# Full attention: the second of two passes over each group of exp pieces moves from VectorE to GpSimd

## The chip, the cores and the metric

The kernel runs on one core of one Trainium2 chip. The metric is the device time of one execution in microseconds (us), as a median over runs. Before the change it is 1766.3 us (3 runs, 1759.68 to 1770.49).

Engine names in the profile: PE is TensorE (PEld its weight loads), DVE is VectorE, ACT is ScalarE, POOL is GpSimd, SP is SyncE.

## The reference

Four layers alternate, each with a layer norm in front and a residual: a sliding local attention (A) and a full attention with one shared key/value head (B). The change touches only B:

```python
def _B_ref(x, wq, wk, wv, wo):          # S = 2048, D = 512, H = 32, Dh = 16
    q = (x @ wq).reshape(B, S, H, Dh)   # ... transposed to heads first
    k = x @ wk                          # one head for all
    v = x @ wv
    scores = einsum("bhqd,bkd->bhqk", q, k) * (Dh ** -0.5)
    p = softmax(scores, axis=-1)
    o = einsum("bhqk,bkd->bhqd", p, v)
    return (...) @ wo
# x = x + A(norm(x)); x = x + B(norm(x)); and both once more
```

Each B layer needs 32 x 2048 x 2048 exponentials. On 128 partitions that is 2048 pieces of 512 columns a layer, 4096 in all.

## The kernel before

TensorE writes scores to PSUM, the memory in which this kernel's matmuls leave their results. Two engines share the exponentials:

- ScalarE takes two pieces in one exp instruction (1024 columns), and TensorE multiplies each by the values: two matmuls a piece (score, value).
- VectorE makes a cheap exponential from bit patterns. A *copy* clamps the score, adds a bias and stores it as int16, and these bits, read as fp16, are roughly 2^x. For four pieces together (a *group*, 2048 columns) two *passes* add a constant to those int16 numbers. TensorE then multiplies the copy and both pass results by values with three different weights, and the sum is a good exponential. A VectorE piece costs four matmuls (a score, three values).

```python
NJ = 3
J_OFF = (0.0, OCT / 3, 2 * OCT / 3)          # OCT = 1024
...
class AttnB:
    def exp(self, key, slot, pt, n):
        self.chain("act", self.nc.scalar.activation(out=self.pt[pt][:, 0:n, :], in_=self.st.pop(key)[:, 0:n, :],
                                                    func=AF.Exp, scale=E_SCALE))
    def copy(self, bank, buf, r):
        self.chain("dve", self.nc.vector.tensor_scalar(out=self.t[buf][:, r, :].bitcast(I16), in0=self.dv[bank][:],
                                                       scalar1=-U_BIAS, scalar2=U_BIAS, op0=ALU.max, op1=ALU.add))
    def do_pass(self, buf, out, j, n):
        self.chain("dve", self.nc.vector.tensor_scalar(out=self.i[out][:, 0:n, :].bitcast(I16),
                                                       in0=self.t[buf][:, 0:n, :].bitcast(I16), scalar1=J_OFF[j],
                                                       scalar2=None, op0=ALU.add))
```

Who takes which piece, and the order on every engine, is fixed when the kernel is built. A planner walks through the stage with a table of durations, always issues what can start first, and `chain` pins the planned order. The durations are constants in the source:

```python
class Stream:
    def copy(self, s, _):
        ...
        S.run("dve", s, 600.0)
        ...
        if len(self.filling) == self.GROUP or ...:
            for j in range(1, NJ):
                self.passes.append((s + 600, buf, j, tiles))
    def do_pass(self, s, _):
        _, buf, j, tiles = self.passes.pop(0)
        t = 133.5 * n + 66
        S.run("dve", s, t)
        ...
```

So the planner decides how many pieces go to ScalarE and how many to VectorE. If a duration in the table is wrong, the kernel stays correct, but the division and the order are wrong.

## Time and profile before

| | before |
|---|---|
| median time | 1766.3 us |
| two full-attention stages (first to last pass) | 670 + 663 us |
| VectorE / ScalarE busy, of 550 us inside the first stage | 536.7 / 531.5 us |
| exp instructions; copies; passes (VectorE / GpSimd) | 1382; 1332; 668 / 0 |

The head of the page (busy time, share of the span, instructions) and its part 4, the chain that ended last:

```profile
span 1772.6 us, 39835 instructions
PE 1569.5 (89%) x16214; PEld 539.7 (30%) x16281; DVE 1535.8 (87%) x2565; ACT 1507.3 (85%) x1721; POOL 206.2 (12%) x257
...
DVE 59%; PE 26%; ACT 9%; issue 3%; POOL 1%; DMA 0%; DVEq 0%; SPq 0%; ACTq 0%; POOLq 0%
DVE t L1103 32%; DVE i L1107 17%; PE o L1118 9%; PE ps L882 5%; PE st L1084 4%; ACT pt L1099 4%; PE dv L1084 3%; DVE P L951 2%; DVE X L1135 2%; DVE stats L857 2%; ACT P L950 1%; PE pv L910 1%; DVE x_sb L1001 1%; PE dn L980 1%; PE o L961 1%
...
L1099 ACT ACTIVATE pt<-st 128x1024 bf16<-128x1024 f32 x1382 | 1290.7, 1094 | 48.2 <-PE dv L1084 20.4
L1103 DVE TENSOR_SCALAR t<-dv 128x512 int16<-128x512 f32 x1332 | 856.9, 680 | 11.3 <-PE dv L1084 6.2
L1107 DVE TENSOR_SCALAR i<-t 128x2048 int16<-128x2048 int16 x668 | 466.0, 698 | 11.2 <-PE o L1118 0.5
```

L1103 is the copy and L1107 the pass; together they are half of the chain, so VectorE sets the pace. The three group lines give, left of the second bar, busy time in us and the mean duration of one in ns; right of it stands the idle time before them. VectorE idles 11 us before copies and 11 us before passes. ScalarE idles 48 us before its exps, so it is close behind. Busy time is less than count times mean (for the exps 1290.7 against 1382 x 1.094 = 1512 us), because the records of consecutive instructions overlap.

The table of windows, from 250 to 800 us, inside the first full-attention stage (columns: us, then busy time and count of each engine, granted TensorE clock as a share of full speed, DMA share, GB/s):

```profile
core 0: us, PE busy (x) PEld busy (x) DVE busy (x) ACT busy (x) POOL busy (x), PEclk, DMA share, GB/s
250.00:800.00 550.00, 519.34 (x4452) 144.80 (x4458) 536.71 (x891) 531.46 (x568) 27.96 (x41) 0.94 0.06 11
```

VectorE is busy 98% of this window, ScalarE 97%. GpSimd is nearly free.

The timelines of GpSimd and VectorE near the end (start us, duration us, engine, line) show that the two engines can get in each other's way already here:

```profile
1730.74 1.27 POOL L1188 TENSOR_TENSOR onc<-X,lb 128x512 bf16<-128x512 f32 x1 [6.37 <-DMA lb<-rd]
...
1729.10 0.68 DVE L1107 TENSOR_SCALAR i<-t 128x2048 int16<-128x2048 int16 x1
1729.70 1.28 DVE L1103 TENSOR_SCALAR t<-dv 128x512 int16<-128x512 f32 x2
1731.01 1.55 DVE L1107 TENSOR_SCALAR i<-t 128x2048 int16<-128x2048 int16 x1
```

The pass at 1731.01 us lasts 1.55 us in place of 0.68. GpSimd's product had begun just before and ended at 1732.01 us; the pass ends 0.55 us after that. The trace books the wait as part of the instruction. What VectorE waits for is called the port from here on; the prediction below says what it is.

The line that I used to cost the new GpSimd work is this one, from the groups of GpSimd by shape. It is the layer norm's normalisation, `x * rstd + nmr`, two operations:

```profile
L871 POOL TENSOR_SCALAR xn<-x_bf,rstd,nmr 128x512 bf16<-128x512 bf16 x9 | 6.8, 768 | 21.8 <-issue 12.5 <-PE pT L875 8.9 <-ACT xnT L845 0.5
```

### The profile page before, as it was taken

Reading aid. Unit: us, or ns where it says so; the run is one execution under the profiler, and the core shown is the slowest. Engines: PE = TensorE matmul, PEld = TensorE weight load, DVE = VectorE, ACT = ScalarE, POOL = GpSimd, SP = SyncE. Lnnn points to the kernel's source line nnn. Section 1 sums busy time; section 2 is a strip of 40 time slices with the busy share of each in tenths; the row PEclk is TensorE's granted clock in tenths of the full one; section 3 lists DMA queues with packets and bytes.
Section 4 is the critical chain, followed back from the end, with each engine's and each line's share of the span. In section 5 each row is a group of like instructions: output and inputs, shape, how many; then the busy total and the mean of one; then the engine's idle time right before and its main releaser. Section 6 shows DMA issues by size and latency. Waiting matters only on the chain.

```text
span 1772.6 us, 39835 instructions
## 1 busy us (share of the span) xinstructions
PE 1569.5 (89%) x16214; PEld 539.7 (30%) x16281; DVE 1535.8 (87%) x2565; ACT 1507.3 (85%) x1721; POOL 206.2 (12%) x257
## 2 busy tenths in 40 slices
PE   5776799899999999999977777998999999999996
PEld 3544222222222223222345442222222222222222
DVE  6565499999999999998955646999999999999997
ACT  4654599999999989999856546999999999999994
POOL 4343000000000000000123420000000000000001
PEclk9988799999988999978998878999999899998998
DMA  4000000000000000000000000000000000000000
GB/s 123 3 2 3 0 5 12 17 11 10 12 11 11 11 11 11 11 11 11 11 2 3 2 2 1 11 11 11 11 11 23 11 11 11 23 14 11 11 15 30
DMA packets 40736, 22.96 MB, mean 13 GB/s; under 512 B 28512, under 2 KB 34272, under 8 KB 40544
## 3 DMA queue, kind: packets, MB, share of 16 engines
q1 hardware_dynamic: 39680, 18.50, 4.8%
q8 instruction: 129, 2.11, 0.5%
q10 hardware_dynamic: 864, 1.84, 0.3%
q14 instruction: 63, 0.52, 0.1%
HBM read 13.27 MB, written 2.59 MB: 9 GB/s over the span
## 4 chain that ended last, share of the span: by engine, by line
DVE 59%; PE 26%; ACT 9%; issue 3%; POOL 1%; DMA 0%; DVEq 0%; SPq 0%; ACTq 0%; POOLq 0%
DVE t L1103 32%; DVE i L1107 17%; PE o L1118 9%; PE ps L882 5%; PE st L1084 4%; ACT pt L1099 4%; PE dv L1084 3%; DVE P L951 2%; DVE X L1135 2%; DVE stats L857 2%; ACT P L950 1%; PE pv L910 1%; DVE x_sb L1001 1%; PE dn L980 1%; PE o L961 1%
## 5 line engine op out<-in xcount | busy, mean ns | idle before, releaser
L1099 ACT ACTIVATE pt<-st 128x1024 bf16<-128x1024 f32 x1382 | 1290.7, 1094 | 48.2 <-PE dv L1084 20.4
L1103 DVE TENSOR_SCALAR t<-dv 128x512 int16<-128x512 f32 x1332 | 856.9, 680 | 11.3 <-PE dv L1084 6.2
L1084 PE MATMUL st<-QT,KAB 32*128 32x512 bf16 x2764 | 560.3, 400 | 14.8 <-ACT pt L1099 13.2
L1084 PE MATMUL dv<-QT,KAB 32*128 32x512 bf16 x1332 | 512.9, 397 | 52.2 <-DVE t L1103 38.4
L1118 PE MATMUL o<-pt,VEa 128*32 128x512 bf16 x2764 | 546.3, 412 | 2.7 <-DVE t L1103 1.8
L1118 PE MATMUL o<-i,VEd 128*32 128x512 f16 x2664 | 535.7, 403 | 10.5 <-DVE i L1107 10.1
L1107 DVE TENSOR_SCALAR i<-t 128x2048 int16<-128x2048 int16 x668 | 466.0, 698 | 11.2 <-PE o L1118 0.5
L1084 PEld LDWEIGHTS <-KAB 32*128 32x128 bf16 x4096 | 188.1, 91 | 556.4 <-issue 541.5
L1118 PE MATMUL o<-t,VEd 128*32 128x512 f16 x1332 | 344.7, 407 | 0.2
L1118 PEld LDWEIGHTS <-VEd 128*32 128x32 f16 x3996 | 145.4, 94 | 225.0 <-issue 221.7
L1118 PEld LDWEIGHTS <-VEa 128*32 128x32 bf16 x2764 | 120.2, 94 | 191.9 <-issue 188.9
L753 POOL TENSOR_TENSOR chk_b<-chk_b,S 128x32 f32<-128x32 f32 x30 | 11.0, 367 | 813.6 <-DMA S<-X 684.3
L951 DVE TENSOR_TENSOR P<-P,bandmask 128x1152 bf16<-128x1152 bf16 (+1 forms) x64 | 60.9, 951 | 38.4 <-ACT P L950 37.8
L950 ACT ACTIVATE P<-s 128x1152 bf16<-128x1152 f32 (+1 forms) x64 | 71.8, 1121 | 16.7 <-PE s L945 16.6
L882 PE MATMUL ps<-xnT,w_sb 128*128 128x512 bf16 x233 | 69.2, 427 | 16.8 <-DVE k L898 8.8
L875 PE MATMUL pT<-ident,xn 128*128 128x128 bf16 x256 | 30.6, 263 | 40.4 <-ACT xn L867 23.2
L1188 POOL TENSOR_TENSOR onc<-X,lb 128x512 bf16<-128x512 f32 x30 | 39.8, 1327 | 228.2 <-DMA lb<-rd 214.5
L984 ACT ACTIVATE logs<-dn 128x512 f32<-128x512 f32 x32 | 19.1, 598 | 45.4 <-PE dn L980 45.2
L961 PE MATMUL o<-P,V 64*32 64x72 bf16 (+2 forms) x2176 | 34.9, 209 | 18.9 <-DVE P L951 15.3
L1135 DVE COPY X<-o 128x512 f32<-128x512 f32 x64 | 43.7, 683 | 8.7 <-PE o L1118 8.6
L986 DVE TENSOR_TENSOR onc<-o,rec 128x512 bf16<-128x512 f32 x32 | 22.0, 687 | 33.0 <-ACT rec L985 24.9
L747 POOL TENSOR_TENSOR logs<-logs 128x512 f32<-128x512 f32 x32 | 34.3, 1071 | 130.1 <-ACT rec L985 130.1
(108 smaller groups left out, 871.1 us busy)
## 6 DMA issues: line engine op xcount, KB each, us to landing
lb<-rd SPq DMA_DIRECT2D x240, 32.0 KB, 1.8
S<-X SPq DMA_DIRECT2D x240, 2.0 KB, 1.7
X<-X SPq DMA_DIRECT2D x120, 32.0 KB, 2.0
rd<-R SPq DMA_DIRECT2D x120, 4.0 KB, 1.5
w_sb<-in_A_wqkv_dram ACTq DMA_DIRECT2D x4, 384.0 KB, 5.6
x_bf<-in_A_x_dram SPq DMA_DIRECT2D x3, 512.0 KB, 9.3
out_dram<-xo SPq DMA_DIRECT2D x3, 512.0 KB, 3.0
x_bf<-in_A_x_dram SPq DMA_DIRECT2D x2, 256.0 KB, 5.0
```

The costliest lines, as they stand in the source:

```text
L857: nc.vector.bn_stats(out=stats[:, i, :], in_=src(i))
L882: self.nc.tensor.matmul(ps[:], lhsT=wcols(kt), rhs=xnT[:, kt, :], start=(kt == 0), stop=(kt == 3))
L950: nc.scalar.activation(out=P[:, :, 0:ncol], in_=st[:, :, 0:ncol], func=AF.Exp, scale=DH ** -0.5)
L951: nc.vector.tensor_tensor(out=P[:, :, 0:ncol], in0=P[:, :, 0:ncol], in1=self.w.band[:, 0:ncol].unsqueeze(1).to_broadcast([128, 4, ncol]), ...
L961: nc.tensor.matmul(o[32 * r:32 * r + 32, q0:q0 + w], lhsT=vv[64 * a:64 * a + 64, kb, t, gh, j, :], rhs=P[64 * a:64 * a + 64, g, col:col + ...
L1084: self.chain("pe", self.nc.tensor.matmul(out, lhsT=self.KAB[32 * g:32 * g + 32, a, kt * 128:(kt + 1) * 128], rhs=self.QT[32 * g:32 * g + 3 ...
L1099: self.chain("act", self.nc.scalar.activation(out=self.pt[pt][:, 0:n, :], in_=self.st.pop(key)[:, 0:n, :], func=AF.Exp, scale=E_SCALE))
L1103: self.chain("dve", self.nc.vector.tensor_scalar(out=self.t[buf][:, r, :].bitcast(I16), in0=self.dv[bank][:], scalar1=-U_BIAS, scalar2=U_B ...
L1107: self.chain("dve", self.nc.vector.tensor_scalar(out=self.i[out][:, 0:n, :].bitcast(I16), in0=self.t[buf][:, 0:n, :].bitcast(I16), scalar1 ...
L1118: self.chain("pe", self.nc.tensor.matmul(self.o[bank][32 * g:32 * g + 32, :], lhsT=lhsT, rhs=rhs, start=first, stop=last, tile_position=(0 ...
L1135: self.chain("dve", nc.vector.tensor_copy(out=self.X[qc, t, a][:], in_=self.o.pop(bank)[:]))
L1188: self.chain("pool", nc.gpsimd.tensor_tensor(out=self.onc[qc][:, t, :], in0=self.X[qc, t, 0][:], in1=bufs["lb"][:], op=ALU.mult))
```

## The change

The intent: VectorE bounds the stage, so take one of its two passes away. Pass 1 stays on VectorE, pass 2 runs on the idle GpSimd, ordered behind pass 1 of the same group. The planner learns a cost for GpSimd's pass (0.86 ns a column plus 250 ns: 2.01 us for a group), keeps the two kinds of pass from overlapping (`port`), gets an ageing term in its priority, and there are seven buffers for pass results in place of five. Cut to its core:

```diff
+POOL_COL = 0.86
...
-                yield (s + op.prio, s, op.ready, self.issue, (e, op))
+                yield (s + op.prio - 0.1 * (s - op.ready), s, op.ready, self.issue, (e, op))
...
-            for j in range(1, NJ):
-                self.passes.append((s + 600, buf, j, tiles))
+            self.passes.append((s + 600, buf, 1, tiles))
...
-        t = 133.5 * n + 66
-        S.run("dve", s, t)
+        t = 133.5 * n + 66 if e == "dve" else POOL_COL * 512 * n + 250
+        S.run(e, s, t)
+        self.port = s + t
+        if j < NJ - 1:
+            self.pool_passes.append((s + t + LAT["dve"], buf, j + 1, tiles))
...
-        self.i = [... for n in range(5)]
+        self.i = [... for n in range(7)]
...
+        eng = self.nc.vector if e == "dve" else self.nc.gpsimd
+        i = eng.tensor_scalar(out=self.i[out][:, 0:n, :].bitcast(I16), in0=self.t[buf][:, 0:n, :].bitcast(I16),
+                              scalar1=J_OFF[j], scalar2=None, op0=ALU.add)
+        if e == "pool":
+            order_after(self.tc, i, self.first_pass.pop(buf))
```

More of the change, by code (lines that the diff above doesn't have):

```diff
@@ L572, in __init__ @@
         self.pos = 0
-        self.exps, self.copies, self.passes = [], [], []
+        self.exps, self.copies, self.passes, self.pool_passes = [], [], [], []
+        self.port = 0.0
         self.res = res
@@ L622, in cands @@
             if self.passes:
-                s = max(S.now["dve"], self.passes[0][0], S.free_at(("i", "vec")))
+                s = max(S.now["dve"], self.passes[0][0], S.free_at(("i", "vec")), self.port)
                 if s < FAR:
-                    yield (s + (0.0 if self.run_of_copies >= 2 else B["pass"]), s, 0.0, self.do_pass, None)
+                    yield (s + (0.0 if self.run_of_copies >= 2 else B["pass"]), s, 0.0, self.do_pass, "dve")
+        elif e == "pool" and self.pool_passes:
+            s = max(S.now["pool"], self.pool_passes[0][0], S.free_at(("i", "vec")), self.port)
+            if s < FAR:
+                yield (s, s, self.pool_passes[0][0], self.do_pass, "pool")
     def fill_slot(self, s, _):
@@ L689, in copy, with do_pass @@
             self.uses[("t", buf)] = [len(tiles) + NJ - 1, 0.0, ("t", "vec")]
-            for j in range(1, NJ):
-                self.passes.append((s + 600, buf, j, tiles))
+            self.passes.append((s + 600, buf, 1, tiles))
             for r, tl in enumerate(tiles):
                 self.queue(tl, done, ("t", buf, r, 0), 1)
-    def do_pass(self, s, _):
+    def do_pass(self, s, e):
         S, io = self.s, self.io
-        _, buf, j, tiles = self.passes.pop(0)
+        _, buf, j, tiles = (self.passes if e == "dve" else self.pool_passes).pop(0)
         n = len(tiles)
-        t = 133.5 * n + 66
-        S.run("dve", s, t)
+        t = 133.5 * n + 66 if e == "dve" else POOL_COL * 512 * n + 250
[3 more added lines that the diff above has]
+            self.pool_passes.append((s + t + LAT["dve"], buf, j + 1, tiles))
         out = S.take(("i", "vec"))
         self.uses[("i", out)] = [n, 0.0, ("i", "vec")]
-        S.note(s, lambda: io.do_pass(buf, out, j, n))
-        self.run_of_copies = 0
+        S.note(s, lambda: io.do_pass(e, buf, out, j, n))
+        if e == "dve":
+            self.run_of_copies = 0
         for r, tl in enumerate(tiles):
-            self.queue(tl, s + t + LAT["dve"], ("i", out, r, j), j < NJ - 1)
+            self.queue(tl, s + t + LAT[e], ("i", out, r, j), j < NJ - 1)
         self.use(("t", buf), s + t)
@@ L1063, in __init__ @@
         self.t = [fixed.tile([128, Stream.GROUP, 512], F16, name=f"t{n}") for n in range(3)]
-        self.i = [fixed.tile([128, Stream.GROUP, 512], F16, name=f"i{n}") for n in range(5)]
+        self.i = [fixed.tile([128, Stream.GROUP, 512], F16, name=f"i{n}") for n in range(7)]
         self.NQC = S // 512
@@ L1074, in __init__ @@
         self.X, self.onc, self.onb, self.xo = {}, {}, {}, {}
-        self.sums, self.ready = {}, {}
+        self.sums, self.ready, self.first_pass = {}, {}, {}
     def chain(self, key, inst):
@@ L1104, in copy, with do_pass @@
                                                        scalar1=-U_BIAS, scalar2=U_BIAS, op0=ALU.max, op1=ALU.add))
-    def do_pass(self, buf, out, j, n):
-        self.chain("dve", self.nc.vector.tensor_scalar(out=self.i[out][:, 0:n, :].bitcast(I16),
-                                                       in0=self.t[buf][:, 0:n, :].bitcast(I16), scalar1=J_OFF[j],
-                                                       scalar2=None, op0=ALU.add))
+    def do_pass(self, e, buf, out, j, n):
+        eng = self.nc.vector if e == "dve" else self.nc.gpsimd
[3 more added lines that the diff above has]
+            order_after(self.tc, i, self.first_pass.pop(buf))
+        else:
+            self.first_pass[buf] = i
+        self.chain(e, i)
     def pv(self, bank, at, src, first, last):
```

## The prediction

> **What bounds the kernel now.** The two attention stages run (source views) from about 209 to 882 us and 1087 to 1752 us, some 1340 of 1773 us. In 250 to 800 us the table of windows shows VectorE busy 536.7 of 550 us, ScalarE 531.5, TensorE 519.3 (overlapping matmuls), GpSimd 28. The chain of waits in the second stage is nearly all VectorE: copies (L1103) 32%, passes (L1107) 17% of the span. So VectorE is first, ScalarE about 1% behind. Costs from the groups: a two-piece exp (L1099) 1290.7/1382 = 0.934 us of ScalarE; a copy 856.9/1332 = 0.643 us; a pass 466.0/668 = 0.698 us.
>
> **What changes.** From the compiled order: exps 1382 to 1340; VectorE pieces 1332 to 1416; 354 passes stay on VectorE, 354 go to GpSimd (668 on VectorE before). 84 pieces take four matmuls in place of two: +168 of 10856, 1.5%.
> - VectorE: +84 x 0.643 = +54 us, -314 x 0.698 = -219 us: -165 us. It stops being the limit.
> - ScalarE: -42 x 0.934 = -39 us (1291 to 1252). It becomes the limit. That, not the 165 us, can be gained: at the present 96 to 97% occupancy the stages take about 1300 us.
> - GpSimd: no such pass in this trace. Its 512-column tensor_scalar (L871) takes 0.768 us. The Trainium skill, "GPSIMD Engine Reference", 3.1, states 1.03 cycles per element for a body of at most two operations: 1.76 us for 2048 columns. With a fixed part fitted to L871 (0.33 us) I estimate 2.1 us, up to 2.5 us if L871's growth is steeper: about 740 of 1300 us.
>
> **The shared port.** The Trainium skill, "SBUF — State Buffer", "SBUF: two separate sides", says GpSimd and a two-port VectorE instruction lock each other out entirely. This trace agrees: the pass at 1731.01 us took 1.55 us because a GpSimd product (1.27 us) had begun at 1730.7; the median is 0.683. Copies out of PSUM never lengthened (623 to 693 ns), so they run beside GpSimd. The ordering makes VectorE's pass and GpSimd's alternate: a group has about 1300/354 = 3.67 us, the passes need 0.7 + 2.1 + hand-over, about 3.1 us.. The reciprocals (L1169), SBUF to SBUF, may now wait for GpSimd: 30 times, about 1 us, mostly absorbed.
>
> **TensorE.** At full clock it has slack; at half clock (about a tenth of the time) four matmuls take 0.545 us and the timeline at 506 to 512 us shows TensorE setting the pace (an exp per 1.09 us). There the extra 1.5% costs a few us.
>
> **Time.** About 38 us gained of 1766: 1729 us, 8 in 10 between 1702 and 1770. Faster by over 2%: 0.50; within 2%: 0.41; slower: 0.09.
>
> **What would show it.** Right: VectorE busy falls by about 150 us; ScalarE idles little and leads the chain in both attention stages; exps 1340 at the same mean; GpSimd passes of 2.0 to 2.5 us; VectorE passes mostly near 0.68 us. Wrong: many VectorE passes of 1.5 us and more (lock); matmuls o<-i waiting for GpSimd; ScalarE idle behind TensorE.
>
> **What would make it wrong.** A GpSimd pass of 2.8 us or more: TensorE's fixed order was planned with a shorter one, so matmuls wait, score tiles come late and ScalarE starves; the gain could vanish. GpSimd runs in order: its product (L1188) behind a late DMA would now hold up passes. More throttling with denser matmuls. On the other side, ScalarE at 98 to 99% would bring 1710 us.

## The result, and the profile after

The changed kernel takes 2645.0 us (4 runs, 2644.64 to 2645.48); before takes 1768.4 us in the same rounds. The ratio is 1.4954, with a 95% interval from 1.4899 to 1.5008. Ratios here are the mean time of one kernel's fast runs over that of the other's of the same rounds, so not quite the ratio of the medians that are quoted.

The page after, the same parts:

```profile
span 2642.9 us, 40768 instructions
PE 2110.3 (80%) x16449; PEld 511.4 (19%) x16449; DVE 2315.3 (88%) x2335; ACT 1567.7 (59%) x1679; POOL 2131.9 (81%) x611
...
DVE 40%; PE 25%; issue 19%; POOL 11%; ACT 3%; DMA 0%; SPq 0%; POOLq 0%; DVEq 0%; ACTq 0%
...
L1117 POOL TENSOR_SCALAR i<-t 128x2048 int16<-128x2048 int16 x354 | 1899.3, 5365 | 237.2 <-DVE i L1117 191.4
L1108 ACT ACTIVATE pt<-st 128x1024 bf16<-128x1024 f32 x1340 | 1351.3, 1025 | 827.7 <-PE st L1093 532.7
L1117 DVE TENSOR_SCALAR i<-t 128x2048 int16<-128x2048 int16 x354 | 1160.4, 3278 | 11.8
...
L1112 DVE TENSOR_SCALAR t<-dv 128x512 int16<-128x512 f32 x1416 | 884.5, 676 | 71.8 <-PE o L1132 30.3
```

The counts are those of the prediction: 1340 exps, 1416 copies, 354 passes on each engine. GpSimd's pass takes 5.37 us, and VectorE's pass 3.28 us on average where it took 0.70. Fewer than before though they are, VectorE's passes fill 1160 us. ScalarE idles 828 us before its exps, most of it until a score matmul ends (533 us). The copies are as long as before (676 ns).

The durations from the source view (minimum/median/maximum in ns, then first and last start in us):

```profile
L1117 DVE TENSOR_SCALAR i<-t x354: 693/3642/4574, 212.1 to 2612.5; 128x2048 int16<-128x2048 int16 x177
L1117 POOL TENSOR_SCALAR i<-t x354: 5356/5362/5807, 213.0 to 2616.3; 128x2048 int16<-128x2048 int16 x177
```

GpSimd's 5.36 us is almost the same every time. A wait inside it would scatter, as VectorE's does. The timelines of VectorE and GpSimd show the rhythm:

```profile
506.93 2.46 DVE L1112 TENSOR_SCALAR t<-dv 128x512 int16<-128x512 f32 x4
509.42 3.65 DVE L1117 TENSOR_SCALAR i<-t 128x2048 int16<-128x2048 int16 x1
512.99 2.46 DVE L1112 TENSOR_SCALAR t<-dv 128x512 int16<-128x512 f32 x4
...
507.16 5.36 POOL L1117 TENSOR_SCALAR i<-t 128x2048 int16<-128x2048 int16 x1
513.23 5.36 POOL L1117 TENSOR_SCALAR i<-t 128x2048 int16<-128x2048 int16 x1 [0.70 <-DVE i L1117]
```

GpSimd holds from 507.16 to 512.52 us. VectorE does its four copies beside it, reaches its pass at 509.42, and finishes it at 513.07, 0.55 us after GpSimd is done. Then the ordering lets GpSimd begin, at 513.23. A group takes 513.23 - 507.16 = 6.07 us. And 354 groups of 6.07 us are 2149 us, against 2180 us for the two stages (from 212.1 to 1302.6 and from 1522.6 to 2612.5 us, the first and last passes of each in the source view by window). So this alternation accounts for the stages almost completely. They lasted 1333 us before; the 847 us between are nearly all of the 870 us by which the span grew. Most of this growth needs no alternation: GpSimd's passes alone, 354 of 5.36 us, are busy for 1899 us, 566 us more than the two stages had lasted. Taking turns with VectorE adds the other 6.07 - 5.36 = 0.71 us a group, about 251 us.

The window inside the first stage:

```profile
250.00:800.00 550.00, 447.28 (x2808) 82.16 (x2803) 516.75 (x475) 346.56 (x346) 499.73 (x113) 0.62 0.03 7
```

TensorE was granted 0.62 of its clock, against 0.94 before, while it had less to do per microsecond (2808 matmuls against 4452).

### The profile page after: what moved, and what is told of

It is laid out like the page before. It is cut to its first block, busy times and chain, and to the rows that moved or that the text cites. A ratio compares the mean times of both kernels' runs of the same rounds, so it can differ in the third digit from the quotient of the medians.

```text
span 2642.9 us, 40768 instructions
## 1 busy us (share of the span) xinstructions
PE 2110.3 (80%) x16449; PEld 511.4 (19%) x16449; DVE 2315.3 (88%) x2335; ACT 1567.7 (59%) x1679; POOL 2131.9 (81%) x611
## 4 chain that ended last, share of the span: by engine, by line
DVE 40%; PE 25%; issue 19%; POOL 11%; ACT 3%; DMA 0%; SPq 0%; POOLq 0%; DVEq 0%; ACTq 0%
DVE t L1112 21%; DVE i L1117 14%; POOL i L1117 10%; PE o L1132 9%; PE st L1093 5%; PE ps L891 3%; PE dv L1093 3%; DVE P L960 1%; DVE X L1149 1%; ACT P L959 1%; PE y L1219 1%; DVE stats L866 1%; DVE x_sb L1010 1%; PE pv L919 1%; PE dn L989 1%
## 5 line engine op out<-in xcount | busy, mean ns | idle before, releaser
L1117 POOL TENSOR_SCALAR i<-t 128x2048 int16<-128x2048 int16 x354 | 1899.3, 5365 | 237.2 <-DVE i L1117 191.4
L1108 ACT ACTIVATE pt<-st 128x1024 bf16<-128x1024 f32 x1340 | 1351.3, 1025 | 827.7 <-PE st L1093 532.7
L1117 DVE TENSOR_SCALAR i<-t 128x2048 int16<-128x2048 int16 x354 | 1160.4, 3278 | 11.8
L1132 PE MATMUL o<-i,VEd 128*32 128x512 f16 x2832 | 862.3, 563 | 156.4 <-POOL i L1117 154.3
L1112 DVE TENSOR_SCALAR t<-dv 128x512 int16<-128x512 f32 x1416 | 884.5, 676 | 71.8 <-PE o L1132 30.3
L1093 PE MATMUL dv<-QT,KAB 32*128 32x512 bf16 x1416 | 701.8, 542 | 257.8 <-DVE t L1112 224.6
L1132 PE MATMUL o<-pt,VEa 128*32 128x512 bf16 x2680 | 777.8, 559 | 0.5 <-DVE t L1112 0.5
L1093 PE MATMUL st<-QT,KAB 32*128 32x512 bf16 x2680 | 737.4, 548 | 0.3 <-ACT pt L1108 0.2
L1132 PE MATMUL o<-t,VEd 128*32 128x512 f16 x1416 | 534.4, 563 | 0.0
L1093 PEld LDWEIGHTS <-KAB 32*128 32x128 bf16 x4096 | 151.0, 97 | 921.6 <-issue 916.6
```

Of the source, the lines that this page charges most:

```text
L1093: self.chain("pe", self.nc.tensor.matmul(out, lhsT=self.KAB[32 * g:32 * g + 32, a, kt * 128:(kt + 1) * 128], rhs=self.QT[32 * g:32 * g + 3 ...
L1117: i = eng.tensor_scalar(out=self.i[out][:, 0:n, :].bitcast(I16), in0=self.t[buf][:, 0:n, :].bitcast(I16), scalar1=J_OFF[j], scalar2=None, ...
L1132: self.chain("pe", self.nc.tensor.matmul(self.o[bank][32 * g:32 * g + 32, :], lhsT=lhsT, rhs=rhs, start=first, stop=last, tile_position=(0 ...
```

## The experiments

Runs marked as single are one execution of unknown state. The differences read from them are far larger than the per cents between states.

### e1_pool_alone: GpSimd's instruction by itself

The kernel before, with GpSimd instructions on scratch tiles at its end, three of each form, when nothing else runs.

```diff
+        G.tensor_scalar(out=int16[2048], in0=int16[2048], scalar1=682.0, scalar2=None, op0=ALU.add)   # also 1024, 512;
+                                                                        # f16, bf16, f32, mixed types
+        G.tensor_scalar(..., scalar1=w.nhalf[:, 0:1], scalar2=w.nhalf[:, 1:2], op0=ALU.mult, op1=ALU.add)   # bf16
+        G.tensor_scalar(..., scalar1=2.0, scalar2=682.0, op0=ALU.mult, op1=ALU.add)                         # int16
+        G.tensor_tensor(out=int32[1024], in0=int32[1024], in1=int32[1024], op=ALU.add)                      # also 512, f32
```

> The kernel before, with GpSimd instructions on scratch tiles added at the end, three of each form, when all other engines are idle. The question is why GpSimd's pass took 5.36 us in the changed kernel where I estimated 2.1 us. Theory A, the instruction itself is that slow: int16 add of a constant over 2048 columns takes 5.3 to 5.4 us here too, 1024 columns about 2.7 us, 512 about 1.4 us. Theory B, it is slowed by the busy VectorE beside it: it takes 2.0 to 2.6 us here. Within A: if it is the 16-bit integer type that costs, bf16 and f32 at 2048 columns take about 2.0 to 3.1 us; if every such instruction grows that steeply, they take about 5.3 us as well. An int32 tensor_tensor add over 1024 columns (two int16 elements in each) should take about 2.35 us, worked out from 0.250 us at 32 columns and 1.265 us at 512 columns of f32 tensor_tensor in the trace of before.

The groups of GpSimd by shape:

```profile
L1428 POOL TENSOR_SCALAR pdst<-psrc 128x2048 int16<-128x2048 int16 x3 | 16.1, 5368 | 0.2
L1428 POOL TENSOR_SCALAR pdst<-psrc 128x2048 bf16<-128x2048 bf16 x3 | 16.1, 5364 | 0.2
L1428 POOL TENSOR_SCALAR pdst<-psrc 128x512 int16<-128x512 int16 x3 | 4.5, 1487 | 0.2
L1438 POOL TENSOR_TENSOR pdst<-psrc,psr 128x1024 int32<-128x1024 int32 x3 | 7.0, 2337 | 0.2
L1434 POOL TENSOR_SCALAR pdst<-psrc,nhalf 128x2048 bf16<-128x2048 bf16 x3 | 6.1, 2049 | 0.3
L1431 POOL TENSOR_SCALAR pdst<-psrc 128x2048 int16<-128x2048 int16 x3 | 5.7, 1898 | 0.3
```

Theory A holds: the pass takes 5.37 us with every other engine idle, so VectorE does not slow it. The type does not matter either; f16, f32 and the mixed forms came to 5.364 us too. What matters is something that I had not written down as a theory: the last two lines, with a multiply and an add, take 2.05 us (bf16, scalars from memory) and 1.90 us (int16, constants). The instruction that does more is nearly three times as fast. The trace of before held only that form (L871).

### e2_no_order: the changed kernel without the order between the two passes

```diff
-        if e == "pool":
-            order_after(self.tc, i, self.first_pass.pop(buf))
-        else:
-            self.first_pass[buf] = i
```

> The changed kernel without the order between VectorE's pass and GpSimd's pass of the same group. In the changed kernel a group takes 6.07 us: GpSimd's 5.36 and VectorE's pass of about 0.6 with a hand-over of 0.1. Theory A, the two passes exclude each other whatever the order: 5.36 + 0.6 stay in series, some 5.97 to 6.07 us a group, 2600 to 2660 us in all, VectorE's passes still about 3 us long. Theory B, the wait ordered between them is what puts them in series: without it GpSimd runs back to back at 5.36 us a group, 177 groups a stage, about 250 us less in all, near 2390 us, and VectorE's passes at 0.7 us.

It took 2559.5 us (single). The source view, and the group of GpSimd's passes on its page:

```profile
L1117 DVE TENSOR_SCALAR i<-t x354: 693/3340/4577, 210.0 to 2527.8; 128x2048 int16<-128x2048 int16 x177
L1117 POOL TENSOR_SCALAR i<-t x354: 5354/5780/5867, 210.1 to 2530.6; 128x2048 int16<-128x2048 int16 x177
...
L1117 POOL TENSOR_SCALAR i<-t 128x2048 int16<-128x2048 int16 x354 | 2004.4, 5675 | 50.7 <-DVE t L1112 44.2
```

Neither range was hit, but the mechanism of A is there: without any ordered wait VectorE's passes still have a median of 3.34 us, and now GpSimd's are stretched too (5.78 us). The two exclude each other by themselves. The order cost 86 us over 354 groups, about 0.24 us a group; the hand-over in the trace above (513.07 to 513.23, 0.16 us) is only a part of that. GpSimd now idles 51 us before its passes, against 237 us with the order: it works almost without a pause, and its own passes of over 5 us set the time.

### e3_true_plan: the changed kernel, planned with GpSimd's real cost

```diff
-POOL_COL = 0.86
+POOL_COL = 2.5
```

> The changed kernel planned with GpSimd's real cost (2.5 ns a column in place of 0.86). The planner then gives VectorE 1042 pieces in place of 1416, ScalarE 1528 exps, GpSimd 262 passes. Theory A, GpSimd's pass and the excluded VectorE pass bound the stage at 6.07 us a group: 262 x 6.07 = 1590 us for both stages, 430 us for the rest: about 2020 us (1980 to 2070), still slower than before. Theory B, it was the stale plan (matmuls waiting in a wrong order) that cost the time: with a right plan the kernel comes to the time of before or below, 1720 to 1790 us.

It took 2113.9 us (single), above the range of A and far from B. The planner gave GpSimd 262 passes, and they still lasted 5.36 us. The two stages lasted 1653 us (first to last pass), 63 us more than the 262 x 6.07 = 1590 us that I had put down. GpSimd's wait of 202 us for VectorE's ordered pass does not explain them, since 262 x 0.70 = 183 us of it lie within the 6.07 us a group; where they come from was not taken apart. The chain that ended last is led here by TensorE (43%) and ScalarE (39%), so the alternation is not the only limit in this run. A stale plan thus made the loss larger (2645 against 2114 us), but this plan, which knows the real duration, did not come near 1768 us. No other plan was tried.

### e4_rest_only: the ageing term and the buffers, both passes on VectorE

```diff
-                yield (s + op.prio, s, op.ready, self.issue, (e, op))
+                yield (s + op.prio - 0.1 * (s - op.ready), s, op.ready, self.issue, (e, op))
...
-        self.i = [... for n in range(5)]
+        self.i = [... for n in range(7)]
```

> The rest of the change alone: the ageing term in the planner's priority and seven buffers for the pass results, both passes on VectorE. Exps (1382) and VectorE pieces (1332) come out as before. Theory A, these parts cost nothing: within 1% of before, 1752 to 1786 us. Theory B, the new order of issue has a share in the slowdown: over 1800 us.

1781.4 us against 1771.5 us, ratio 1.0044 (1.0008 to 1.0081). These parts cost about half a per cent and do not explain the slowdown.

### e6_two_ops: GpSimd's pass as two additions

From e1 I concluded that two operations are fast and one is slow. The cheapest second operation is to add zero.

```diff
-                              scalar1=J_OFF[j], scalar2=None, op0=ALU.add)
+                              scalar1=J_OFF[j], scalar2=0.0, op0=ALU.add, op1=ALU.add)     # on GpSimd only
```

> The changed kernel with GpSimd's pass written as two operations, add the offset and then add 0.0, which gives the same numbers. Measured alone, int16 over 2048 columns takes 1.898 us with two constant operations and 5.364 us with one. Nothing else is changed, so the plan and the counts (1340 exps, 1416 VectorE pieces, 354 passes on each engine) are those of the changed kernel. Theory A, the wrong duration of this pass was the only step that failed, and the rest of the prediction holds: 1729 us (1705 to 1755), VectorE passes mostly near 0.68 us, GpSimd passes 1.9 us, mean granted clock back at 0.90 to 0.93, ScalarE the limit. Theory B, taking turns at the shared port costs the gain also with the short pass (VectorE waits in its queue, matmuls wait for GpSimd): 1765 us or more, VectorE passes at 1.5 us and above, many of them.

It took 3255.0 us, ratio 1.8376 (1.8316 to 1.8435). The group of GpSimd's passes:

```profile
L1118 POOL TENSOR_SCALAR i<-t 128x2048 int16<-128x2048 int16 x354 | 2507.5, 7083 | 238.7 <-DVE i L1118 201.3 <-PE o L1133 19.7 <-PE dv L1093 13.2
```

A miss of my own making. Each pass takes 7.08 us, longer than with one operation. My conclusion from e1 changed two things at once, the number of operations and their kinds. Both theories that I had stated assumed a pass of 1.9 us, so this run tests neither. It does give another point for the alternation: the pass is 7.08 - 5.37 = 1.71 us longer than in the changed kernel, over 354 groups about 605 us, and the kernel is 3255 - 2645 = 610 us longer. Its companion, e7_two_ops_no_order, the same without the order, had this on record:

> The two-operation version without the order between VectorE's pass and GpSimd's. GpSimd may then begin just before VectorE's pass of the same group and hold the port for 1.9 us. Theory A, the order protects VectorE: without it many VectorE passes take 1.5 to 2.5 us, and the time is 1% to 3% above the ordered version. Theory B, the order is of no use once the pass is short, or costs its hand-over: the same time within 0.5% or a little less.

It took 3163.4 us, ratio 1.7866. It rests on the same wrong assumption; as in e2, the order costs time (92 us) when GpSimd sets the pace.

### e5_packed: two int16 elements added as one int32

The numbers are not negative and small enough that the lower half never carries into the upper one. The output stays correct.

```diff
+            i = self.nc.gpsimd.tensor_tensor(out=self.i[out][:, 0:n, :].bitcast(I32),
+                                             in0=self.t[buf][:, 0:n, :].bitcast(I32),
+                                             in1=<a constant tile of pairs of 683>, op=ALU.add)
```

> The changed kernel with GpSimd's pass as an int32 tensor_tensor add over 1024 columns, two int16 elements in each, with a constant tile. Measured alone it takes 2.337 us. The plan still holds 2.01 us for it. It tells whether the 16 per cent that the pass is longer than planned matter. Theory A, only a pass that no longer fits into the group's time (3.67 us less VectorE's 0.7) hurts: within 1% of the two-operation version, 1720 to 1765 us. Theory B, TensorE's order is so tight that 0.33 us more each group come through: about 50 to 115 us over the two-operation version.

1737.4 us, ratio 0.9816 (0.9773 to 0.9859). Passes of 2.35 us, with everything else as in the changed kernel. The time lies in theory A's range. Its comparison, the two-operation version, had failed; the short pass that came later (e8) is about 1% faster by the ratios.

### e8_mult_add: multiply by one, then add

```diff
+        if e == "dve":
+            ops = dict(scalar1=J_OFF[j], scalar2=None, op0=ALU.add)
+        else:
+            ops = dict(scalar1=1.0, scalar2=J_OFF[j], op0=ALU.mult, op1=ALU.add)
```

> The changed kernel with GpSimd's pass as multiply by 1.0, then add the offset, which gives the same numbers. The version with add, add took 7.08 us a pass in the kernel; multiply, add over 2048 int16 columns took 1.898 us alone. So the pair of operations, not their number, sets the duration. Nothing else is changed from the changed kernel: same plan, same counts. Theory A, only the duration of this pass failed in the prediction: passes of 1.9 us on GpSimd, 1729 us (1705 to 1750), at or a little below the packed version (1737 us, passes of 2.35 us), clock 0.90 to 0.95. Theory B, what the multiply, add form saved alone is lost beside a busy VectorE: GpSimd's passes over 3 us, time over 1768 us.

1725.1 us (6 runs, 1722.88 to 1727.64) against 1773.9 us, ratio 0.9714 (0.9684 to 0.9744). It is the fastest version in this study, and it differs from the changed kernel in this one instruction. From its page (the chain by line, then a group), its source view and its window:

```profile
DVE t L1112 22%; ACT pt L1108 16%; PE o L1135 13%; PE st L1093 8%; PE ps L891 5%; PE dv L1093 5%; DVE P L960 2%; DVE stats L866 2%; DVE i L1121 2%; ACT P L959 1%; PE y L1222 1%; DVE x_sb L1010 1%; PE pv L919 1%; PE dn L989 1%; PE o L970 1%
...
L1108 ACT ACTIVATE pt<-st 128x1024 bf16<-128x1024 f32 x1340 | 1245.9, 1100 | 37.9 <-PE dv L1093 15.5 <-PE st L1093 14.5 <-PE o L1135 3.7
...
L1121 DVE TENSOR_SCALAR i<-t x354: 630/694/1905, 211.0 to 1701.4; 128x2048 int16<-128x2048 int16 x177
L1121 POOL TENSOR_SCALAR i<-t x354: 1897/1897/2337, 211.9 to 1702.2; 128x2048 int16<-128x2048 int16 x177
...
250.00:800.00 550.00, 522.92 (x4773) 146.96 (x4772) 506.70 (x811) 537.66 (x581) 309.18 (x193) 0.99 0.06 12
```

GpSimd's pass takes 1.90 us. VectorE's pass is back at a median of 0.69 us. In the window ScalarE is busy 537.7 of 550 us and VectorE 506.7: by busy time the limit has changed from VectorE to ScalarE, as intended. The chain does not show it as clearly: the copies have 22% of it and the exps 16%, so the prediction's sign "leads the chain in both attention stages" did not come. The granted clock is 0.99.

### e9_mult_add_no_order: the same without the order

```diff
-            order_after(self.tc, i, self.first_pass.pop(buf))     # and the bookkeeping for it, as in e2
```

> The multiply, add version without the order between VectorE's pass and GpSimd's. Without the order the slow form gained 86 us (2645 to 2559), about 0.24 us a group, because GpSimd was the bottleneck and began earlier. With passes of 1.9 us GpSimd is not the bottleneck. Theory A, the order protects VectorE: without it many VectorE passes wait for the port and take 1.5 to 2.5 us, time 1% to 3% above the ordered version. Theory B, VectorE has slack and absorbs it: within 0.7% of the ordered version.

1742.4 us, ratio 0.9815 (0.9775 to 0.9854), so 1% above the ordered version: theory A in time, at the edge of its range. But its picture was wrong. VectorE's passes keep a median of 694 ns; it is GpSimd's that are stretched, to a median of 2.40 us. The order is worth 17 us when the pass is short, and it cost 86 us when the pass was long.

### e10_forms: which pairs of operations are fast

As e1, constants, int16 over 2048 columns, one line for each form.

> The kernel before, with GpSimd tensor_scalar forms on scratch tiles at the end, other engines idle, int16 over 2048 columns, constants. Known: add 5.364 us, multiply then add 1.898 us, and add then add 7.08 us in a kernel. Theory A, multiply then add is a special fast path and every other form is slow: multiply alone, subtract, add then multiply, multiply then subtract about 5.4 (one operation) or 7.1 us (two). Theory B, add as the first operation is what is slow: multiply alone and multiply then anything take 1.7 to 2.1 us, add first or subtract first 5.3 us or more. Over 1024 and 512 columns multiply then add should take about 1.0 and 0.6 us if it grows by 0.86 ns a column.

```profile
L1450 POOL TENSOR_SCALAR pdst<-psrc 128x2048 int16<-128x2048 int16 x3 | 21.3, 7089 | 0.2
...
L1448 POOL TENSOR_SCALAR pdst<-psrc 128x2048 int16<-128x2048 int16 x3 | 16.1, 5366 | 0.2
L1458 POOL TENSOR_SCALAR pdst<-psrc 128x2048 int16<-128x2048 int16 x3 | 5.7, 1898 | 0.2
L1452 POOL TENSOR_SCALAR pdst<-psrc 128x2048 int16<-128x2048 int16 x3 | 5.7, 1897 | 0.2
...
L1460 POOL TENSOR_SCALAR pdst<-psrc 128x512 int16<-128x512 int16 x1 | 0.6, 618 | 0.1
```

L1450 is add, add; L1448 multiply alone; L1458 multiply, add; L1452 add, multiply; L1460 multiply, add over 512 columns. The complete result:

| form | us |
|---|---|
| add; subtract; multiply (one operation) | 5.372; 5.368; 5.366 |
| add, add; multiply, subtract; multiply, max | 7.089; 7.089; 7.079 |
| multiply, add; add, multiply | 1.898; 1.897 |

Neither theory fits entirely. One multiply and one add, in either order, are fast; all six other forms tried are slow, and then two operations cost 1.7 us more than one. The fast form grows by (1898 - 618) / 1536 = 0.83 ns a column, the single add by (5368 - 1487) / 1536 = 2.53 ns (e1). Why GpSimd treats that pair differently no run here shows.

### e11_both_gpsimd: both passes on GpSimd, in the fast form

```diff
-            self.passes.append((s + 600, buf, 1, tiles))
+            for j in range(1, NJ):
+                self.pool_passes.append((done, buf, j, tiles))
...
-        t = 133.5 * n + 66 if e == "dve" else POOL_COL * 512 * n + 250
+        t = 133.5 * n + 66 if e == "dve" else POOL_COL * 512 * n + 140
```

It starts from e9, without an order.

> Both passes of a group on GpSimd, in the multiply, add form, none on VectorE, so that no VectorE pass can meet GpSimd at the port. The planner then gives 1390 exps to ScalarE (1340 in the multiply, add version with one pass moved), 1316 pieces to VectorE, 660 passes to GpSimd. GpSimd: 660 x 1.9 = 1254 us of some 1330; ScalarE: 1390 x 0.934 = 1298 us. Theory A, what counts is how much ScalarE is relieved: 50 exps more than the one-pass version cost some 47 us, so 1760 to 1785 us, no better than before. Theory B, taking turns at the port was costing the one-pass version much: 1725 us or less.

1810.9 us, ratio 1.0236 (1.0196 to 1.0276). Theory B is out, and A's range was too low:

```profile
L1111 DVE TENSOR_SCALAR t<-dv 128x512 int16<-128x512 f32 x1316 | 822.1, 682 | 318.1 <-POOL i L1120 207.3 <-PE dv L1092 73.0 <-PE o L1130 19.1
```

The copies on VectorE now wait 207 us for GpSimd, which sets the pace together with ScalarE (each busy 529 of 550 us in the window from 250 to 800 us). Of the plans that this planner made, one pass on each engine is the better division.

## Why the prediction was wrong

**The step that failed** is the cost of GpSimd's pass: "With a fixed part fitted to L871 (0.33 us) I estimate 2.1 us, up to 2.5 us if L871's growth is steeper: about 740 of 1300 us." Measured: 5.36 us, 1899 us busy. L871 multiplies and adds; the pass only adds. I matched engine and instruction name and scaled up the column count, but did not match the operations, and took for granted that fewer operations can't cost more. For the form that I had measured, the estimate was right: over 2048 columns it takes 2.05 us with scalars from memory, 1.90 us with constants (e1). The figure that I took from the Trainium skill, "GPSIMD Engine Reference", 3.1, 1.03 cycles an element for a body of at most two operations, agrees with the multiply and add pair (0.83 ns a column is 1.0 cycle at the page's 1.2 GHz) and not with the single add (2.53 ns, 3.0 cycles). The page gives it for a loop body and names no instruction; that it holds for this one was my assumption.

**What followed from it** is the next step: "a group has about 1300/354 = 3.67 us, the passes need 0.7 + 2.1 + hand-over, about 3.1 us." With 2.1 us that fits. With 5.36 us a group takes 6.07 us, as the trace shows. GpSimd's pass alone is longer than the 3.67 us that a group had, so by this sum GpSimd would have set the pace even without the port (1899 us against 1333 us). The port adds VectorE's pass to each round, and VectorE stands still behind it.

**Right, point by point.**
- The exclusion, for which I cited the Trainium skill, "SBUF — State Buffer", "SBUF: two separate sides". VectorE's passes end 0.55 us after GpSimd's in the trace after, and e2 shows it without any ordered wait. Copies out of PSUM are not held up (676 ns, 680 before), also as predicted.
- The counts and the value of the change, given a short pass. With the pass at 1.90 us and nothing else changed, the kernel takes 1725 us (predicted 1729) and ScalarE becomes the busiest engine. The gain is about 49 us (predicted 38) of the 165 us taken from VectorE on paper. That the two times agree within 4 us is in part luck: the pass is shorter than the 2.1 us of the prediction, and the kernel before took 1774 us in these rounds, not 1766. The packed version (2.35 us) takes 1737 us, 34 us less than the kernel before in its rounds.
- The warning, in part: "A GpSimd pass of 2.8 us or more" would spoil it. But I expected the loss from TensorE's order and said that "the gain could vanish". In fact matmuls waited for GpSimd's results 154 us, while VectorE's passes were lengthened by about 354 x (3.28 - 0.70) = 913 us. My list of signs did name this, "many VectorE passes of 1.5 us and more (lock)", but I gave it too little weight: the upper end of my range was 1770 us.

**Wrong as well:** "More throttling with denser matmuls." The denser stream of e8 ran at a granted clock of 0.99, the sparser one of the changed kernel at 0.62. The Trainium skill, "TensorE: Matmul & The Clock Gate", Part 1, says that the clock halves after idle windows and returns with activity; the direction agrees with these numbers (in the window TensorE idles 103 of 550 us in the changed kernel, 31 before), but no run here shows the rule itself. Since e8 differs from the changed kernel only in GpSimd's instruction, the low clock is a result of the slow pass, not the first cause. Whether it then added to the time no run separates; the groups' 6.07 us leave little for it to explain.

**Open:** why GpSimd is fast for one pair of operations, and how the kernel would behave with a slow pass on GpSimd if VectorE's pass did not use the shared port.

## What to carry to other kernels

Cost an operation that moves to another engine with exactly its own form: the same operations, not only the same instruction, type and size, and if the trace has none, run it alone first; that took one run here. Multiply it by its count and compare that with the stage first: 354 passes of 5.36 us could not fit into 1333 us. When two engines exclude each other, add their durations for each round of work, and compare the sum with the time a round has: below it the kernel still gained here (e5, e8), above it the sum became the period of the whole stage (the changed kernel, e6). And after a bad result look for the wrong number before giving up the idea: one changed instruction turned 2645 us into 1725 us.

## What the Trainium skill lacked or had wrong

- "GPSIMD Engine Reference", 3.1: 1.03 cycles an element is given for a body of at most two operations. Alone on the chip, multiply with add grows by 0.83 ns a column (1.0 cycle), but a single add, subtract or multiply takes 5.37 us for 2048 columns (2.53 ns a column for the add, 3.0 cycles), and add with add, multiply with subtract and multiply with max 7.08 to 7.09 us. The page does not name these cases.
- "GPSIMD Engine Reference", 4.1: one-input work is called roughly line-rate. A one-input, one-operation add over 2048 columns took 5.37 us on GpSimd, and a two-input add of 2048 f16 columns took less, 4.05 us.
- "GPSIMD Engine Reference", 4.1, on exact integer adds, lacks their use for packed 16-bit numbers: an int32 add of 1024 columns (2048 int16 numbers) took 2.34 us.
- "SBUF — State Buffer", "SBUF: two separate sides", does not say how the lock looks in a trace when VectorE waits: the wait is counted into the duration of the waiting instruction (a VectorE pass of 0.69 us shows as 3.64 us).
